# The transposed g through DRAM, probabilities normalised on GpSimd, and spread w_out steps in an attention and soft-MoE kernel

## The chip, the core and the metric

The kernel runs on one core of a Trainium2 chip. The metric is the device time of one execution in microseconds (us); smaller is better. The five engines of a core work side by side, each through its own list of instructions in order: PE (TensorE, matrix products), DVE (VectorE), ACT (ScalarE), POOL (GpSimd) and SP (SyncE, which here only issues DMAs). An instruction that waits holds up everything behind it in its engine's list.

## What is computed

Three layers follow one another. Attention runs within chunks of 64 tokens, for 8 heads of 64; its output x has 4608 tokens of 512. The second layer is a gated product, and the third routes tokens to 32 slots of 8 experts (soft MoE):

```python
attn = softmax(q @ k.T / 8)                      # within each chunk; sum + 1e-9 in the denominator
x = attn @ v
h = x @ w_in;  g = h * sigmoid(1.702 * h);  y = g @ w_out            # 512 -> 2048 -> 512
logits = y @ phi                                                     # 4608 x 32
d = softmax(logits over tokens);  c = softmax(logits over slots)
slot_out = relu((d.T @ y) @ w1[e]) @ w2[e]                           # per expert e
out = c @ slot_out
```

## The kernel before

The tokens are worked in 12 blocks of 384. For each block, `gemm(b, f)` computes 16 tiles of h (index f, 0 to 15), each 128 features by 384 tokens. Operands are split into a high and a low part, so one tile takes 12 matmuls (lines 240, 241, 242). ACT takes the tanh (line 244), and DVE makes `gt` from it (line 245), which holds g with features on partitions.

y is never formed. The logits come from `logits` with w_out and phi multiplied beforehand (line 301, tile `lp`). The slot inputs d.T @ y are gathered as d.T @ g, added into `acc` block by block by `dispatch` (line 398, tile `dtg`, 12 matmuls), and multiplied with w_out once at the end. For that product g must stand with tokens on partitions. DVE transposes each `gt` in squares of 32 by 32 (line 252) into a tile `g1`, one for a group of four f; when a group is complete, 16 DMAs of 48 KB rearrange it, SBUF to SBUF, into `g2` (line 262). Half of them are issued by POOL and half by SP, in the last blocks all by SP. `dispatch(b-1)` in block b reads the four `g2` tiles. The last block transposes on PE instead (`gemm_t`).

Attention for the blocks ahead is worked between the gemm tiles. One step `attn_a` takes 128 tokens: scores on PE (line 178, tile `s`), maximum and subtraction on DVE (183, 184), exponential on ACT (188), sum, small addition and reciprocal on DVE (190, 191, 193), and the multiplication by the reciprocal (194), on DVE for the steps taken here. `attn_b` transposes the result on PE (206) and copies it on ACT (208). `attn_c` multiplies with v on PE (224, tile `x`) and splits the output into `xh` (ACT, 230) and `xl` (DVE, 231), the operands of a later gemm. The PSUM tiles of `s` and `x` share one buffer (`pair_tile`, one buffer), so an `s` waits until the `xl` of the `x` before it is done, and an `x` until the subtraction (184) of the `s` before it.

`conv_wo` turns a 512 KB piece of w_out from float64 to float32: ACT (line 102), then DVE (103, 106). `load_wo` loads the next piece by SP (line 409). The two take turns.

What stands after which tile is given by the table `PLAN` (`LAST` for the last block): a letter for the step, a number for its part, and the f after which `side` calls it: `l` logits, `s` slots, `a`, `b`, `c` attention, `d` dispatch, `w` one step of w_out. SP issues in program order. The other engines' lists are ordered by a scheduler that estimates when operands are ready, so a step may stand well behind its f there. Tiles of 768 KB come from a pool `slab` of 10 buffers (`xh`, `xl`, `g1`, `g2`, and expert weights towards the end). `TABLE` says when expert weights are loaded into buffers that fall free in blocks 9 to 11.

Of the kernel before, what the change touches and what calls it, by code (L numbers as in the profile page):

```python
# [8 lines left out]
F32 = mybir.dt.float32  # L9
# [11 lines left out]
NM = 8  # L21
NSPARE = 6
NW = 17
NSP = 2
ROOM = {'w': 4, 's': 6, 'q': 4, 'v': 2, 'x': 2, 'p': 6}
TABLE = {'9.13': 'wxx', '10.6': 'q', '10.11': 'vq', '10.15': 'v', '11.0': 'ssw', '11.2': 's', '11.6': 's', 'a': 'ss', 'b': 'ssss', 'e': 'pppppp'}
TABLE.update({f'11.{f}': TABLE.get(f'11.{f}', '') + 'w' for f in range(1, 16)})
EVAC = 'vvvvvvvvvvvvvvaa'
LAST = (('l3', 1), ('s0', 2), ('d0', 4), ('l0', 4), ('s1', 6), ('l1', 8), ('l2', 12))


PLAN = (('l3', 1), ('s0', 2), ('w0', 2), ('a2', 4), ('d0', 4), ('l0', 4), ('b1', 4), ('c0', 4), ('w1', 6), ('s1', 6), ('a3', 8), ('l1', 8), ('b2', 8), ('c1', 8), ('w2', 10), ('w3', 11), ('a4', 12), ('l2', 12), ('b3', 12), ('c2', 12))
NCV = 6
FIRST = "q0 A0 q1 z Li0 A1 q2 Li1 q3 v0 Li2 i0 A2 B0 C0 v1 B1 C1 phi v2 i1 Li3 B2 C2 v3 A3 q4 Li4 i2 Li5 Li6 g0 Li7 g1 i3 Li8 i4 i5 q5 Li9 v4 i6 Li10 g2 g3 Li11 A4 i7 B3 g4 Li12 i8 C3 Lo0r q6 i9 g5 Li13 g6 i10 B4 q7 A5r Li14 i11 g7 o0 g8 i12 i13 g9 Lo1r C4 v5 Lo2r A6r Li15 i14 B5 Lo3 Lo4r i15 o1 g10 C5 g11 g12 g13 o2 Lo5r v6 Lo6 g14 Lo7r Lo8r s o3 g15 G0 o4 Lo9 Lo10r o5 Lo11r o6 G1 Lo12r A7 o7 Lo13r o8 G2 G3 v7 o9 B6 c0 o10 v8 Lo14 G4 o11 o12 C6 d0 G5 o13 c1 t0 Lo15 t1 o14 m0 G6 G7 G8 t2 t3 B7 d1 c2 q8 q9 G9 o15 t4 l0 d2 c3 G10 l1 C7 m1 l2 A8r G11 t5 d3 l3 t6 G12 v9 B8 t7 G13 S t8 G14 D1 t9 t10 t11 C8 t12 G15 T t13 t14 q10 m2 t15 D3 v10 A9 q11 B9 A10 q12"
EPS = 1e-9
# [3 lines left out]
def attention_moe_softmoe_kernel(  # L39
# [12 lines left out]
    nc = tc.nc  # L52
# [6 lines left out]
    NB = NT // T  # L59
# [7 lines left out]
    slab = ctx.enter_context(tc.tile_pool(name="slab", bufs=NSLAB))  # L67
    wpool = ctx.enter_context(tc.tile_pool(name="wpool", bufs=NW))
    mid = ctx.enter_context(tc.tile_pool(name="mid", bufs=NM))
    vpool = ctx.enter_context(tc.tile_pool(name="vpool", bufs=NV))  # L70
    st_p = ctx.enter_context(tc.tile_pool(name="st", bufs=2))
    ps_h = ctx.enter_context(tc.tile_pool(name="ps_h", bufs=3, space=bass.MemoryType.PSUM))
# [8 lines left out]
    def slab_tile(shape, dtype, name):  # L81
        return slab.tile(shape, dtype, tag="s", name=name)
# [153 lines left out]
    def gemm(b, f):  # L236
        h = ps_h.tile([128, T], F32, tag="h", name="h")
        for k in range(KD):
            a, l = w_t[f][:, 0, k, :], w_t[f][:, 1, k, :]
            nc.tensor.matmul(out=h, lhsT=a, rhs=xh[b][:, k, :], start=(k == 0), stop=False)  # L240
            nc.tensor.matmul(out=h, lhsT=a, rhs=xl[b][:, k, :], start=False, stop=False)  # L241
            nc.tensor.matmul(out=h, lhsT=l, rhs=xh[b][:, k, :], start=False, stop=(k == KD - 1))  # L242
        t = mid_tile([128, T], "gt") if b else pro[0].tile([128, T], F32, tag="gt", name="gt", bufs=NF)
        nc.scalar.activation(out=t, in_=h, func=ACTF.Tanh, scale=0.851)  # L244
        nc.vector.scalar_tensor_tensor(out=t, in0=t, scalar=1.0, in1=h, op0=ALU.add, op1=ALU.mult)  # L245
        gt[b, f] = t
        q, j = divmod(f, GF)
        if b in (0, NB - 1):
            return
        if j == 0:  # L250
            g1[q] = slab_tile([128, 4, NCP, GF * 32], F32, "g1")
        nc.vector.transpose(  # L252
            out=g1[q][:, :, :, 32 * j:32 * (j + 1)], in_=t.rearrange("p (a b c) -> p b a c", b=4, c=32)
        )
        if j == GF - 1:
            dst = slab_tile([128, 4, NCP, GF * 32], F32, f"g2_{q}")
            g2.setdefault(b, []).append([dst[:, :, i, :] for i in range(NCP)])
            src = g1.pop(q)
            for fq in range(4):
                for tb in range(4):  # L260
                    eng = nc.gpsimd if tb % 2 and b + NSP < NB else nc.sync
                    eng.dma_start(  # L262
                        out=dst[32 * tb:32 * tb + 32, fq].rearrange("p a c -> p (a c)"),
                        in_=src[32 * fq:32 * fq + 32, tb].rearrange("p a c -> p (a c)"),
                    )

    def gemm_t(b, f, g=None):
        g = gt[b, f] if g is None else g
# [123 lines left out]
    def dispatch(b):  # L392
        dt, cr = dt_t.pop(b)
        g = g2.pop(b)
        p = ps.tile([128, 512], F32, tag="m" if b + 1 < NB else "pt", name="dtg")
        for i in range(NCP):
            for j in reversed(range(4)):
                nc.tensor.matmul(  # L398
                    out=p[32 * j:32 * (j + 1)], lhsT=dt[:, i, :], rhs=g[j][i], start=(i == 0), stop=(i == NCP - 1)
                )  # L400
        nc.vector.scalar_tensor_tensor(out=acc, in0=acc, scalar=cr, in1=p, op0=ALU.mult, op1=ALU.add)
# [36 lines left out]
    def load(kind, eng):  # L438
        room, runs = ROOM[kind], []
        while units and (2 if units[0][0] == 1 else 1) <= room:  # L440
            u = units.pop(0)
            room -= 2 if u[0] == 1 else 1
            if runs and runs[-1][0] == u[:-1] and runs[-1][1] + runs[-1][2] == u[-1]:
                runs[-1][2] += 1
            else:
                runs.append([u[:-1], u[-1], 1])
        if not runs:
            return
        if kind == "x":
            wo_t["x"] = wo_t.get("x", 0) + 1  # L450
            t = wo_t["t"][:, wo_t["x"], :]
        else:
            alloc = {"w": w_tile, "s": slab_tile, "p": spare_tile, "v": v_alloc, "q": q_alloc}[kind]
            t = alloc([128, ROOM[kind] * DH], F32, "w12")
        at, live = 0, set()
        for key, c, m in runs:
            if key[0] == 1:
                v = t[:, at:at + m * DM].rearrange("p (c k f) -> p c k f", c=m, k=KD)
                at += m * DM
                eng.dma_start(out=v, in_=w1[:, key[1], c:c + m])  # L460
                for z in range(m):
# [23 lines left out]

    def at(key):
        for c in TABLE.get(key, ""):
            load(c, nc.gpsimd)

    def tail():  # L490
        b = NB - 1
# [128 lines left out]
    def side(b, f):  # L620
        for name, at in (LAST if b == NB - 1 else PLAN):
            if f != at:
                continue
            kind, i = name[0], int(name[1:])
            if kind == "l":
                if i == NG - 1:
                    logits(b - 1, i)
                else:
                    logits(b, i)
            elif kind == "s":  # L630
                (slots_a, slots_b)[i](b - 1)
            elif kind == "d":
                dispatch(b - 1)
            elif kind == "w":
                if 1 < b < 10:
                    more_wo()
            elif (b + 1) * NCP + i < NB * NCP:
                cp = (b + 1) * NCP + i
                if kind == "a":
                    attn_a(cp)  # L640
                    load_qk(cp + 2)
                elif kind == "b":
                    attn_b(cp)
                else:
                    attn_c(cp)
                    load_v(cp + 2)
# [118 lines left out]
```

## Time and profile before

| | us |
|---|---|
| median of 3 runs | 729.85 (726.99 to 732.1) |
| profiled execution | 733.41 |
| its span, first to last instruction | 731.6 |
| busy within the span: PE | 658.2 |
| DVE | 458.8 |
| ACT | 242.2 |
| POOL | 213.7 |

The granted clock of PE was 0.981 of full speed on average. In the views below a row of the timeline gives start, duration, engine, line, operation, tiles (out<-in), shapes and count, and in brackets the idle time of that engine ahead of it with what ended it. A matmul of float32 operands appears as two instructions, so the 12 of `dispatch` count 24. Successive matmuls overlap, so the time that one takes from PE is read from start to start. Blocks 2 to 11 start at 146.8, 206.4, 255.4, 303.2, 352.5, 401.0, 449.6, 499.2, 548.6 and 593.0 us; from 646 us to the end follow the experts and the output.

### The profile page before, as it was taken

What the parts mean: (1) busy time and instruction counts of PE and PEld (TensorE: products, weight loads), DVE (VectorE), ACT (ScalarE), POOL (GpSimd) and SP (SyncE); (2) the same over time, 40 slices, a digit from 0 to 9 for tenths busy, and PEclk for the clock granted to TensorE, in tenths of its full rate; (3) what the DMA queues carried; (4) which work ended last, traced back from release to release, by engine and by line L of the source; (5) the groups of instructions that cost most, each with busy time, mean ns of one, the idle gap of its engine ahead of it and who ended that gap; (6) DMA issues with size and microseconds to landing.
All of it is one profiled execution on the core that took longest, in us unless ns stands there. A gap on an engine that the chain in (4) does not pass through costs nothing.

```text
span 731.6 us, 17216 instructions
## 1 busy us (share of the span) xinstructions
PE 658.2 (90%) x6862; PEld 535.6 (73%) x6862; DVE 458.8 (63%) x988; ACT 242.2 (33%) x517; POOL 213.7 (29%) x400
## 2 busy tenths in 40 slices
PE   3878999999899999998999999989999988988873
PEld 2777976667796978887879788869687976846542
DVE  6798672658577686677777866767677544331033
ACT  4556344523332333323333333233233221121132
POOL 1335021222323342424232424242332023145410
PEclk9988999999999999999999999999999999999998
DMA  7846274254444645544446355444563366779996
GB/s 248 316 177 228 87 223 153 59 173 120 113 130 125 168 109 151 159 129 115 132 132 179 92 163 167 136 118 129 122 196 87 100 212 190 248 237 394 405 378 260
DMA packets 55216, 129.14 MB, mean 177 GB/s; under 512 B 14176, under 2 KB 25440, under 8 KB 55136
## 3 DMA queue, kind: packets, MB, share of 16 engines
q1 hardware_dynamic: 35568, 75.59, 33.1%
q0 software_dynamic: 19568, 52.45, 22.7%
q8 instruction: 54, 0.88, 0.5%
q14 instruction: 26, 0.21, 0.1%
HBM read 87.10 MB, written 9.44 MB: 132 GB/s over the span
## 4 chain that ended last, share of the span: by engine, by line
PE 64%; DVE 13%; DMA 9%; issue 4%; SPq 4%; ACT 4%; POOL 0%; DVEq 0%; ACTq 0%
PE h L240 13%; PE h L241 12%; PE h L242 12%; DMA wo<-in_moe_w_out_dram 5%; PE dtg L398 4%; PE lp L301 4%; SPq L262 4%; PE x L224 3%; DVE gt L245 2%; DMA g<-g 2%; PE h1p L555 2%; PE fp L575 2%; PE s L178 2%; PE op L603 2%; PE pt L206 2%
## 5 line engine op out<-in xcount | busy, mean ns | idle before, releaser
L240 PE MATMUL h<-xh,w 128*128 128x384 f32 x768 | 268.3, 350 | 0.7 <-ACT xh L230 0.7
L242 PE MATMUL h<-xh,w 128*128 128x384 f32 x768 | 260.5, 339 | 0.0
L241 PE MATMUL h<-xl,w 128*128 128x384 f32 x768 | 260.5, 339 | 0.0
L262 POOL DMA_DIRECT2D g<-g x288 | 141.2, 498 | 327.4 <-issue 101.5
L244 ACT ACTIVATE gt<-h 128x384 f32<-128x384 f32 x192 | 93.0, 489 | 212.9 <-PE h L242 212.1
L240 PEld LDWEIGHTS h<-xh,w 128*128 128x128 f32 x768 | 146.5, 191 | 14.0 <-issue 9.4
L245 DVE SCALAR_TENSOR_TENSOR gt<-gt,h 128x384 f32<-128x384 f32 x192 | 104.6, 545 | 74.7 <-ACT gt L244 74.0
L241 PEld LDWEIGHTS h<-xl,w 128*128 128x128 f32 x768 | 146.3, 190 | 1.9 <-issue 1.5
L242 PEld LDWEIGHTS h<-xh,w 128*128 128x128 f32 x768 | 146.0, 190 | 0.1
L252 DVE STREAM_TRANSPOSE g<-gt 128x384 f32<-128x384 f32 x160 | 91.9, 575 | 6.2 <-DMA g<-g 2.3
L301 PE MATMUL lp<-gt,wp 128*32 128x384 f32 x384 | 50.5, 496 | 5.5 <-DVE gt L245 5.5
L460 POOL DMA_DIRECT2D w<-in_moe_w_dram x41 | 21.8, 536 | 90.7 <-PE h L242 36.3
L224 PEld LDWEIGHTS x<-pt_sb,v 64*64 64x64 f32 x1152 | 22.4, 145 | 28.8 <-issue 24.4
L224 PE MATMUL x<-pt_sb,v 64*64 64x64 f32 x1152 | 27.0, 236 | 18.2 <-issue 9.3
L188 ACT ACTIVATE e<-e 128x512 f32<-128x512 f32 x36 | 22.7, 631 | 57.2 <-DVE e L184 57.2
L398 PE MATMUL dtg<-g,dt 128*32 128x512 f32 x264 | 32.3, 622 | 7.9 <-DVE gt L245 2.7
L178 PE MATMUL s<-qk 64*64 64x64 f32 x1152 | 27.5, 237 | 12.3 <-DMA qk<-in_qk_dram 7.9
L178 PEld LDWEIGHTS s<-qk 64*64 64x64 f32 x1152 | 22.3, 146 | 21.9 <-issue 15.1
L183 DVE TENSOR_REDUCE mx<-s 128x8 f32<-128x512 f32 x36 | 24.1, 669 | 17.8 <-PE s L178 17.7
L127 POOL TENSOR_TENSOR w<-cv,w 128x512 fp32r<-128x512 f32 x16 | 21.6, 1357 | 46.1 <-ACT w L126 38.9
L208 ACT ACTIVATE pt_sb<-pt 128x512 f32<-128x512 f32 x36 | 21.5, 596 | 40.2 <-PE pt L206 40.2
L190 DVE TENSOR_REDUCE sm<-e 128x8 f32<-128x512 f32 x36 | 24.5, 681 | 12.0 <-ACT e L188 12.0
(106 smaller groups left out, 607.9 us busy)
## 6 DMA issues: line engine op xcount, KB each, us to landing
w<-in_moe_w_dram POOLq DMA_DIRECT2D x47, 512.0 KB, 7.4
qk<-in_qk_dram SPq DMA_DIRECT2D x36, 512.0 KB, 4.8
g<-g SPq DMA_DIRECT2D x352, 48.0 KB, 2.3
g<-g POOLq DMA_DIRECT2D x288, 48.0 KB, 2.0
v<-in_v_dram SPq DMA_DIRECT2D x36, 256.0 KB, 4.7
stg<-in_moe_w_in_dram SPq DMA_DIRECT2D x16, 512.0 KB, 8.8
stg<-in_moe_w_out_t_dram SPq DMA_DIRECT2D x16, 512.0 KB, 5.2
wo<-in_moe_w_out_dram SPq DMA_DIRECT2D x16, 512.0 KB, 4.5
```

The costliest lines, as they stand in the source:

```text
L178: nc.tensor.matmul(out=p[w, h, hp, :], lhsT=t[r, 0, hp, w], rhs=t[r, 1, hp, w], start=True, stop=True)
L190: nc.vector.tensor_reduce(out=sm, in_=e, axis=AX.X, op=ALU.add)
L224: nc.tensor.matmul(out=x[64 * z:64 * z + 64, h, a, w], lhsT=t[r, 2 * a + z, w], rhs=p[r, 2 * a + z, w], start=True, stop=True,)
L240: nc.tensor.matmul(out=h, lhsT=a, rhs=xh[b][:, k, :], start=(k == 0), stop=False)
L241: nc.tensor.matmul(out=h, lhsT=a, rhs=xl[b][:, k, :], start=False, stop=False)
L242: nc.tensor.matmul(out=h, lhsT=l, rhs=xh[b][:, k, :], start=False, stop=(k == KD - 1))
L244: nc.scalar.activation(out=t, in_=h, func=ACTF.Tanh, scale=0.851)
L245: nc.vector.scalar_tensor_tensor(out=t, in0=t, scalar=1.0, in1=h, op0=ALU.add, op1=ALU.mult)
L252: nc.vector.transpose(out=g1[q][:, :, :, 32 * j:32 * (j + 1)], in_=t.rearrange("p (a b c) -> p b a c", b=4, c=32))
L262: eng.dma_start(out=dst[32 * tb:32 * tb + 32, fq].rearrange("p a c -> p (a c)"), in_=src[32 * fq:32 * fq + 32, tb].rearrange("p a c -> p ( ...
L301: nc.tensor.matmul(out=lp[b][32 * j:32 * (j + 1), :], lhsT=wp[:, f, :], rhs=gt[b, f], start=(g == 0), stop=(g == NG - 1),)
L398: nc.tensor.matmul(out=p[32 * j:32 * (j + 1)], lhsT=dt[:, i, :], rhs=g[j][i], start=(i == 0), stop=(i == NCP - 1))
```

## The change

It makes four edits.

- A complete group of g is written to a DRAM tile by 4 DMAs of 192 KB, all issued by SP (line 259 of the new kernel), in place of 16 DMAs of 48 KB by SP and POOL. A new step `g` (`load_g`) reads all four groups of block b-1 back in block b with 4 DMAs of 768 KB (line 271), tokens on partitions, after f = 3 (after f = 2 in the last block). The `g2` buffers are taken there, no longer as each group completes.
- `dispatch` moves from f = 4 to f = 8 in `PLAN` and from f = 4 to f = 6 in `LAST`.
- The attention steps called from `side` multiply by the reciprocal (line 194) on POOL.
- The w_out steps move from f = 2, 6, 10, 11 to f = 6, 7, 14, 15. In `TABLE`, the loads of block 9 come at f = 15 and from SP, and two slab loads of block 11 at f = 7 in place of f = 2 and f = 6.

```diff
-NSP = 2
-TABLE = {'9.13': 'wxx', ... '11.0': 'ssw', '11.2': 's', '11.6': 's', ...}
+TABLE = {'9.15': 'wxx', ... '11.0': 'ssw', '11.7': 'ss', ...}
-LAST = (('l3', 1), ('s0', 2), ('d0', 4), ('l0', 4), ('s1', 6), ('l1', 8), ('l2', 12))
+LAST = (('l3', 1), ('s0', 2), ('g0', 2), ('l0', 4), ('d0', 6), ('s1', 6), ('l1', 8), ('l2', 12))
-PLAN = (('l3', 1), ('s0', 2), ('w0', 2), ('a2', 4), ('d0', 4), ('l0', 4), ('b1', 4), ('c0', 4), ('w1', 6), ...
+PLAN = (('l3', 1), ('s0', 2), ('g0', 3), ('a2', 4), ('l0', 4), ('b1', 4), ('c0', 4), ('s1', 6), ('w0', 6), ('w1', 7), ...
...
         if j == GF - 1:
-            dst = slab_tile([128, 4, NCP, GF * 32], F32, f"g2_{q}")
-            g2.setdefault(b, []).append([dst[:, :, i, :] for i in range(NCP)])
-            src = g1.pop(q)
+            src, d = g1.pop(q), dram.tile([4, 32, 4, NCP * GF * 32], F32, tag="g", name="g_dram")
+            g_dram[b, q] = d
             for fq in range(4):
-                for tb in range(4):
-                    eng = nc.gpsimd if tb % 2 and b + NSP < NB else nc.sync
-                    eng.dma_start(
-                        out=dst[32 * tb:32 * tb + 32, fq].rearrange("p a c -> p (a c)"),
-                        in_=src[32 * fq:32 * fq + 32, tb].rearrange("p a c -> p (a c)"),
-                    )
+                nc.sync.dma_start(
+                    out=d[:, :, fq, :].rearrange("b p x -> p b x"),
+                    in_=src[32 * fq:32 * fq + 32].rearrange("p b a c -> p b (a c)"),
+                )
+    def load_g(b):
+        g2[b] = []
+        for q in range(NG):
+            t = slab_tile([128, 4, NCP, GF * 32], F32, f"g2_{q}")
+            nc.sync.dma_start(
+                out=t.rearrange("p q a c -> p (q a c)"), in_=g_dram.pop((b, q)).rearrange("b p q x -> (b p) (q x)")
+            )
+            g2[b].append([t[:, :, i, :] for i in range(NCP)])
...
-            load(c, nc.gpsimd)
+            load(c, nc.sync if key[0] == "9" else nc.gpsimd)
...
-                    attn_a(cp)
+                    attn_a(cp, True)
```

How the lists of the engines change is shown at three places of block 3 or 4; every block from 3 to 9 has the same pattern. On PE before, these rows of block 3 stand between the tiles f = 4 and f = 5 (`s` scores, `dtg` dispatch, `lp` logits, `pt` transpose, `x` the product with v):

```order
L178 MATMUL s<-qk 64x64 x16
L398 MATMUL dtg<-g_3_2390,dt 32x512
L398 MATMUL dtg<-g_2_2240,dt 32x512
L398 MATMUL dtg<-g_1_2089,dt 32x512
L398 MATMUL dtg<-g_0_1916,dt 32x512
...
L301 MATMUL lp<-gt,wp 32x384 x4
L206 MATMUL pt<-ident,e 128x128 x4
L224 MATMUL x<-pt_sb,v 64x64 x16
```

In the changed kernel the dispatch of block 3 stands after the tile f = 11, between the second `s` and the second `x` of the block; the third `s` follows after f = 12:

```order
L310 MATMUL lp<-gt,wp 32x384
L178 MATMUL s<-qk 64x64 x16
L407 MATMUL dtg<-g_3_2435,dt 32x512
L407 MATMUL dtg<-g_2_2433,dt 32x512
L407 MATMUL dtg<-g_1_2431,dt 32x512
L407 MATMUL dtg<-g_0_2429,dt 32x512
...
L224 MATMUL x<-pt_sb,v 64x64 x16
...
L178 MATMUL s<-qk 64x64 x16
L310 MATMUL lp<-gt,wp 32x384 x3
L206 MATMUL pt<-ident,e 128x128 x4
```

So the dispatch moved by seven tiles, and the second `s` from after f = 8 to after f = 11. On DVE before, this is what stands in block 3 around that second attention step, from its maximum to the `xl` of the `x` after it:

```order
L183 TENSOR_REDUCE mx<-s 128x8
L184 TENSOR_TENSOR e<-s,mx 128x2x4x64
L190 TENSOR_REDUCE sm<-e 128x8
L191 TENSOR_SCALAR sm<-sm 128x8
L193 RECIPROCAL rs<-sm 128x8
L194 TENSOR_TENSOR e<-e,rs 128x512
L231 TENSOR_TENSOR xl<-x,xh 128x2x2x128
```

In the changed kernel (block 4), two `gt`, three transposes, the addition into `acc` and a third `gt` stand between them, and the multiplication (194) is gone to POOL:

```order
L183 TENSOR_REDUCE mx<-s 128x8
L184 TENSOR_TENSOR e<-s,mx 128x2x4x64
L245 SCALAR_TENSOR_TENSOR gt<-gt,h 128x384 x2
L252 STREAM_TRANSPOSE g_3161<-gt 128x12x32
L190 TENSOR_REDUCE sm<-e 128x8
L252 STREAM_TRANSPOSE g_3161<-gt 128x12x32
L191 TENSOR_SCALAR sm<-sm 128x8
L410 SCALAR_TENSOR_TENSOR acc<-acc,cr,dtg 128x512
L193 RECIPROCAL rs<-sm 128x8
L245 SCALAR_TENSOR_TENSOR gt<-gt,h 128x384
L252 STREAM_TRANSPOSE g_3161<-gt 128x12x32
L231 TENSOR_TENSOR xl<-x,xh 128x2x2x128
```

The `xl` thus moved behind seven other instructions. On SP before, these rows issue the DMAs of block 4 from its first complete group of g on (`qk` and `v` feed attention):

```order
L262 DMA g_0_3111<-g_3021 32x384 x8
L161 DMA qk<-in_qk_dram 128x1024
L167 DMA v<-in_v_dram 128x512
L409 DMA wo_3259<-in_moe_w_out_dram 128x512
L262 DMA g_1_3284<-g_3144 32x384 x8
```

In the changed kernel the same stretch holds four writes, four reads and, after the second group, the load of w_out, whose conversion now stands seven tiles later:

```order
L259 DMA g_dram<-g_2895 32x4x384 x4
L271 DMA g_0_2987<-g_dram 128x1536
L271 DMA g_1_2989<-g_dram 128x1536
L271 DMA g_2_2991<-g_dram 128x1536
L271 DMA g_3_2993<-g_dram 128x1536
L161 DMA qk<-in_qk_dram 128x1024
L167 DMA v<-in_v_dram 128x512
L259 DMA g_dram<-g_3011 32x4x384 x4
L418 DMA wo_3143<-in_moe_w_out_dram 128x512
```

The writes and reads of g stand on SP alone, POOL's list has none of them any more, and the reads stand ahead of the block's `qk` and `v`.

## Rows read from the trace of the kernel before

**Rows 1.** Timeline of PE: start us, us, engine line op, count, [idle]; blocks 3 and 10.

```profile
218.22 0.70 PE L178 MATMUL s<-qk 64*64 64x64 f32 x32
219.36 2.78 PE L398 MATMUL dtg<-g,dt 128*32 128x512 f32 x24 [0.45 <-DVE gt L245]
221.94 0.86 PE L301 MATMUL lp<-gt,wp 128*32 128x384 f32 x8
222.72 0.66 PE L206 MATMUL pt<-ident,e 128*128 128x128 f32 x4
223.31 0.69 PE L224 MATMUL x<-pt_sb,v 64*64 64x64 f32 x32
...
561.61 2.78 PE L398 MATMUL dtg<-g,dt 128*32 128x512 f32 x24 [0.45 <-DVE gt L245]
```

**Rows 2.** Timeline of PE, block 4: the first and the thirteenth of undisturbed gemm matmuls.

```profile
301.16 0.33 PE L240 MATMUL h<-xh,w 128*128 128x384 f32 x1
...
303.24 0.34 PE L240 MATMUL h<-xh,w 128*128 128x384 f32 x1
```

**Rows 3.** Timeline of PE, block 3, after the tile f = 8.

```profile
232.46 0.69 PE L178 MATMUL s<-qk 64*64 64x64 f32 x32
...
234.88 0.83 PE L301 MATMUL lp<-gt,wp 128*32 128x384 f32 x2 [0.95 <-DVE gt L245]
...
237.94 0.69 PE L224 MATMUL x<-pt_sb,v 64*64 64x64 f32 x32 [0.59 <-DVE e L184]
238.57 0.45 PE L240 MATMUL h<-xh,w 128*128 128x384 f32 x1
```

**Rows 4.** Timeline of ACT, same stretch; then waits of blocks 3 to 9 (total, times, longest).

```profile
232.50 0.68 ACT L102 ACTIVATE wo<-wo 128x512 f32<-128x512 f32 x1 [3.60 <-DMA wo<-in_moe_w_out_dram]
...
ACT wo L102 <- DMA wo<-in_moe_w_out_dram: 34.7, 14, 4.0
```

**Rows 5.** Timeline of DVE, block 3: one attention step, then a gemm tile's two.

```profile
236.42 0.65 DVE L183 TENSOR_REDUCE mx<-s 128x8 f32<-128x512 f32 x1
237.10 0.69 DVE L184 TENSOR_TENSOR e<-s,mx 128x512 f32<-128x512 f32 x1
238.49 0.69 DVE L190 TENSOR_REDUCE sm<-e 128x8 f32<-128x512 f32 x1 [0.70 <-ACT e L188]
...
239.69 0.69 DVE L194 TENSOR_TENSOR e<-e,rs 128x512 f32<-128x512 f32 x1
240.30 0.68 DVE L231 TENSOR_TENSOR xl<-x,xh 128x512 fp32r<-128x512 f32 x1
240.90 0.54 DVE L245 SCALAR_TENSOR_TENSOR gt<-gt,h 128x384 f32<-128x384 f32 x1
241.48 0.58 DVE L252 STREAM_TRANSPOSE g<-gt 128x384 f32<-128x384 f32 x1
```

**Rows 6.** PE in block 2; then a window: length, busy (count) of PE, PEld, DVE, ACT, POOL, granted clock, DMA share, GB/s.

```profile
187.55 0.69 PE L224 MATMUL x<-pt_sb,v 64*64 64x64 f32 x32 [3.18 <-issue]
...
188.00:192.00 4.00, 4.00 (x32) 3.93 (x22) 3.44 (x8) 1.27 (x3) 0.00 (x0) 0.61 0.54 182
```

**Rows 7.** Timeline of PE, block 11.

```profile
602.85 0.45 PE L321 MATMUL lg<-lps,sel 128*128 128x384 f32 x1 [2.01 <-DVE lps L313]
...
611.18 4.46 PE L398 MATMUL dtg<-g,dt 128*32 128x512 f32 x24 [2.28 <-DMA g<-g]
```

**Rows 8.** SP's issues on line 262 (ns min/median/max, first to last); window of the weight stream.

```profile
L262 SPq DMA_DIRECT2D g<-g x352: 507/589/2149, 94.8 to 607.8; - x176
...
656.00:692.00 36.00, 31.64 (x526) 19.32 (x518) 4.88 (x17) 3.66 (x10) 18.77 (x36) 1.00 1.02 397
```

**Rows 9.** Groups by line and form: busy us, mean ns, idle before.

```profile
L106 DVE SCALAR_TENSOR_TENSOR cv<-stg,cv 128x512 uint32<-128x512 uint32 x32 | 26.2, 825 | 0.3
...
L106 DVE SCALAR_TENSOR_TENSOR wo<-wo,wo 128x512 uint32<-128x512 uint32 x16 | 10.7, 672 | 0.2
...
L194 POOL TENSOR_TENSOR e<-e,rs 128x512 f32<-128x512 f32 x3 | 4.1, 1354 | 0.0
```

More of the change, by code (lines that the diff above doesn't have):

```diff
@@ L23 @@
 NW = 17
-NSP = 2
 ROOM = {'w': 4, 's': 6, 'q': 4, 'v': 2, 'x': 2, 'p': 6}
-TABLE = {'9.13': 'wxx', '10.6': 'q', '10.11': 'vq', '10.15': 'v', '11.0': 'ssw', '11.2': 's', '11.6': 's', 'a': 'ss', 'b': 'ssss', 'e': 'pppppp'}
+TABLE = {'9.15': 'wxx', '10.6': 'q', '10.11': 'vq', '10.15': 'v', '11.0': 'ssw', '11.7': 'ss', 'a': 'ss', 'b': 'ssss', 'e': 'pppppp'}
 TABLE.update({f'11.{f}': TABLE.get(f'11.{f}', '') + 'w' for f in range(1, 16)})
 EVAC = 'vvvvvvvvvvvvvvaa'
-LAST = (('l3', 1), ('s0', 2), ('d0', 4), ('l0', 4), ('s1', 6), ('l1', 8), ('l2', 12))
-PLAN = (('l3', 1), ('s0', 2), ('w0', 2), ('a2', 4), ('d0', 4), ('l0', 4), ('b1', 4), ('c0', 4), ('w1', 6), ('s1', 6), ('a3', 8), ('l1', 8), ('b2', 8), ('c1', 8), ('w2', 10), ('w3', 11), ('a4', 12), ('l2', 12), ('b3', 12), ('c2', 12))
+LAST = (('l3', 1), ('s0', 2), ('g0', 2), ('l0', 4), ('d0', 6), ('s1', 6), ('l1', 8), ('l2', 12))
+PLAN = (('l3', 1), ('s0', 2), ('g0', 3), ('a2', 4), ('l0', 4), ('b1', 4), ('c0', 4), ('s1', 6), ('w0', 6), ('w1', 7), ('a3', 8), ('d0', 8), ('l1', 8), ('b2', 8), ('c1', 8), ('a4', 12), ('l2', 12), ('b3', 12), ('c2', 12), ('w2', 14), ('w3', 15))
 NCV = 6
@@ L69, in attention_moe_softmoe_kernel @@
     mid = ctx.enter_context(tc.tile_pool(name="mid", bufs=NM))
+    dram = ctx.enter_context(tc.tile_pool(name="dram", bufs=8, space=bass.MemoryType.DRAM))
     vpool = ctx.enter_context(tc.tile_pool(name="vpool", bufs=NV))
@@ L255, in gemm @@
         if j == GF - 1:
-            dst = slab_tile([128, 4, NCP, GF * 32], F32, f"g2_{q}")
-            g2.setdefault(b, []).append([dst[:, :, i, :] for i in range(NCP)])
-            src = g1.pop(q)
+            src, d = g1.pop(q), dram.tile([4, 32, 4, NCP * GF * 32], F32, tag="g", name="g_dram")
+            g_dram[b, q] = d
             for fq in range(4):
-                for tb in range(4):
-                    eng = nc.gpsimd if tb % 2 and b + NSP < NB else nc.sync
-                    eng.dma_start(
-                        out=dst[32 * tb:32 * tb + 32, fq].rearrange("p a c -> p (a c)"),
-                        in_=src[32 * fq:32 * fq + 32, tb].rearrange("p a c -> p (a c)"),
-                    )
+                nc.sync.dma_start(
+                    out=d[:, :, fq, :].rearrange("b p x -> p b x"),
+                    in_=src[32 * fq:32 * fq + 32].rearrange("p b a c -> p b (a c)"),
+                )
+    g_dram = {}
+    def load_g(b):
[6 more added lines that the diff above has]
+            g2[b].append([t[:, :, i, :] for i in range(NCP)])
     def gemm_t(b, f, g=None):
@@ L633, in side @@
                 dispatch(b - 1)
+            elif kind == "g":
+                load_g(b - 1)
             elif kind == "w":
```

## Prediction, made before the changed kernel was run

> **What bounds the kernel now.** I read the busy times first: PE works in 658.2 of 731.6 us, so it sets the end, and an edit is worth only what it takes from PE's work or from its idle time. So I went down PE's timeline from block to block. The dispatch of block 3 starts at 219.36 and that of block 10 at 561.61 [rows 1]: seven equal blocks (3 to 9) in 342.25 us, or 48.9 each.
>
> How much of that is PE's own work? Taken from start to start: twelve undisturbed gemm matmuls take 303.24 - 301.16 = 2.08 [rows 2], so 16 tiles 33.3. Four `lp` take 222.72 - 221.94 = 0.78, four groups 3.1; the four transposes `pt` 0.59, three times 1.8; the dispatch 221.94 - 219.36 = 2.58 [rows 1]. `x` takes 238.57 - 237.94 = 0.63 [rows 3], and `s`, which has as many matmuls and the same busy time, I give as much: three of each 3.8. The `lg` matmuls I put at 0.35 (two instructions of a gemm matmul's size). Sum 44.9, so 4.0 per block are lost.
>
> I looked for the 4.0 in the same rows. Dispatch: from `s` at 218.22 to `x` at 223.31 are 5.09, against 0.63 + 2.58 + 0.78 + 0.59 = 4.58 of work: 0.5 lost, behind a `gt`. After the tile f = 8: from `s` at 232.46 to the next tile at 238.57 are 6.11. Of work stand there `s`, `lp`, `pt`, `x`, and some six more gemm matmuls (1.04): 3.67. So 2.4 are lost [rows 3]. The last 1.0 is small change at f = 12 and between kinds of matmul.
>
> The 2.4 have one cause, seen on ACT: at 232.50 its line 102 has just waited 3.60 us for the DMA of a w_out piece, and in blocks 3 to 9 this wait comes 14 times with 34.7 us in all [rows 4]. ACT's list is in order, so the tanh behind it is late, then `gt` on DVE, then `lp` on PE [0.95]; the maximum of the second attention step starts at 236.42, four us after its `s` began [rows 3, 5], and `x`, which shares the buffer with that `s`, waits for the subtraction.
>
> **The change, part by part.** *The w_out steps.* Load and conversion now stand seven tiles or more apart, over 7 x 2.08 = 14.6 us. The row [rows 4] shows a piece arriving 3.6 us after ACT was ready for it. ACT's wait ends, and with it the 2.4 per block.
>
> *The dispatch.* Its 2.58 stay. What becomes late next? The third `s` stands after the tile f = 12 and needs the buffer of the second `x`, that is, its `xl` on DVE. On PE there lie between the second and the third `s`: dispatch 2.58, `x` 0.63, a tile 2.08, in all 5.3. On DVE, in its new order: maximum 0.68, subtraction 0.69, three `gt` at 0.54, three transposes at 0.58, sum 0.69, the two small operations about 0.5, the addition into `acc` about 0.7 (an operation of 128x512, as line 194), `xl` 0.68 [rows 5]. That is 7.3 if none overlaps the next; the starts in those rows lie 0.03 to 0.1 closer than the durations, so 6.8 to 7.2. PE thus waits 1.5 to 1.9 in a place where it did not; I take 1.6. Bounds: 0.8, if the scheduler's order leaves two small gaps less, and 2.3, if each step starts late by the 0.70 that the sum has behind the exponential [rows 5]. The 0.5 behind `gt` at the old dispatch goes, the small change stays near 0.9.
>
> *POOL's multiplication* takes 1.354 [rows 9] against 0.69 on DVE. It is hidden: it starts when the reciprocal is done, and DVE's third `gt`, transpose and `xl` (1.8) and the third `s` follow before PE comes to the transposes `pt`. Without that cover it costs 1.354 - 0.69 = 0.7, three times a block. POOL is free for it: the g DMAs it issued are gone from its list.
>
> *g through DRAM.* The trace has no DRAM write of this kind. SP issued half of 64 DMAs of g a block, 32, and issues 20 now (four groups of four writes, four reads), at 0.589 a median issue [rows 8]: 7 us less, on an engine that bounds nothing. The reads can be issued once the last group of the block before is transposed and written: about four tiles of work plus four issues into the block, 14 us; the dispatch stands about 31 us into the block. So 17 us for 3.15 MB (four times 768 KB), while the writes, as many bytes again, spread over the rest of the block. The two nearest rates: 397 GB/s in the weight stream [rows 8], by which the reads take 8 us, and 182 GB/s in a busy stretch of block 2 [rows 6], by which they take 17.3. I take the first, since DMAs there were as large as these and the second stretch was not short of DMA (share 0.54). Cost nothing; ends 0 and the case below.
>
> [...]
>
> *Blocks 3 to 9*: 44.9 + 1.6 + 0.9 = 47.4 for 48.9, a gain of 1.5, seven times 10.5.
>
> *Block 2.* Here the stall is 3.18 before an `x`, and in the 4 us behind it the granted clock is 0.61, between the levels 1.2 and 2.4 GHz: [rows 6] PE gave 4 us for 2.44 of work, 1.56 lost. Both go, 0.4 of small change too, and the new wait comes: -3.18 - 1.56 - 0.4 + 1.6 = -3.5.
>
> *Block 10* keeps its dispatch near its end: its last `xl` now stands behind dispatch and transposes on DVE, before the first tile of block 11, 1.1 later, less the 0.5 at the old dispatch: +0.6.
>
> *Block 11.* PE waits 2.01 for `lps` and 2.28 for a g DMA of the last group, after which the dispatch takes 4.46, not 2.78 [rows 7, 1]: 1.7 at the lower clock. The new list puts the dispatch two tiles later and the read of g behind writes that are long done: -2.01 - 2.28 - 1.7 + 0.5 for small waits that remain = -5.5.
>
> *Blocks 0, 1 and the tail*: nothing. Two slab loads of block 11 come up to 5 tiles later, but the stream that they belong to runs at 397 GB/s with PE idle only 4.4 of 36 us there [rows 8].
>
> *Sum*: -10.5 - 3.5 + 0.6 - 5.5 = -18.9. From the profiled 733.4 this is 714.5; the median of the runs is 3.6 below that execution, so 711.
>
> **Rivals.** *A: the new wait is long enough for the clock to fall.* For it: a stall of 3.18 and one of 2.28 shortly behind one of 2.01 were followed by the lower clock [rows 6, 7]. Against it: 2.01 alone was not. If the wait is 2.3 and each is followed by block 2's loss of 1.56, a block costs 2.3 more than I put, over blocks 2 to 9 18: 729, no change. DVE could be slowed by POOL's multiplication: line 106 takes 825 ns in the first blocks and 672 later [rows 9]. The Trainium skill, "SBUF — State Buffer", section "Who interferes with whom", says that a DVE instruction with two SBUF inputs contends with a GpSimd instruction that reads SBUF, and one with at most one does not; `gt`, the subtraction and `xl` have one input in PSUM, so by it this chain isn't touched.
>
> *B, the other side: the g read comes late.* It decides if the reads run under 3.15 MB / 17 us = 185 GB/s. For it: the 182 GB/s above, and that the reads share the DMA engines with qk, v and the writes. At 134 GB/s (about three quarters of it, the other traffic taken off) they take 23.5 us, the dispatch waits 6.2, and 1.6 of clock follow: 7.8 over nine blocks is +70, so 781. Against it: the DMA share of the stretch was half.
>
> *C: the change doesn't do what it says.* The w_out conversion still waits, since the load stands behind g's writes and reads on SP, which wait for DVE. Then the 2.4 stay beside the new 1.6, less the 0.5 and 0.1 of the rest: +1.0 in each of blocks 2 to 9, +0.6 in block 10 and -5.5 in block 11, so about 3 above before, 733. Against it: seven tiles, 14.6 us, are more than the SP list holds there.
>
> *D: the g traffic starves the expert weights* of block 11 and the tail: the reads and writes of the last two blocks, 6.3 MB at 397 GB/s, push 16 us of the stream; if half shows, 719; if all, 727 or more.
>
> **How the numbers follow.** The forecast has 0.66, A 0.13, B 0.11, C 0.06, D 0.04. The likeliest case's own range, with the wait at 0.8 or 2.3 in eight blocks (-6.4, +5.6) and the block 11 gain halved (+2.7), is 704 to 719. With A and D in and B out, the range is 703 to 730. A measurement of this kernel can tell about 1% (7.3 us) from no change. Faster than 722.5 are the forecast and half of D, with part of A: 0.70; within 1% the rest of A, C and D, and a B that is barely late: 0.18; slower 0.12, from B and a tail of D.
>
> **What would show it.** Right: ACT's wait on line 102 for the w_out DMA gone in blocks 3 to 9; blocks of about 47.4; PE's third `s` waiting 1.5 to 1.9 for DVE's `xl`, with the granted clock at 1.00 behind it; no `dtg` waiting for a DMA; block 11's waits of 2 us and the 4.46 gone. Wrong: a `dtg` that waits for g from DRAM (B); a granted clock under 0.7 behind the third `s` (A); line 102 still waiting (C); PE idle on expert weights behind 646 us (D); or `pt` waiting for POOL's multiplication, which I hold hidden.

## The result and the profile after

| | us |
|---|---|
| median of 4 runs, changed | 722.28 (721.42 to 722.89) |
| median of 4 runs, before, same chip | 729.49 |
| ratio | 0.990, 95% interval 0.9863 to 0.9937 |
| profiled execution, changed | 722.78 (before: 733.41) |
| its span | 721.0 (before: 731.6) |

The change makes the kernel 1% faster. The forecast was 711, with 703 to 730 as the range: the sign is right, the gain is 7 us where 18.9 were forecast. The profiled executions differ by 10.6, more than the medians, since the one before lay 3.9 above its median.

The page of the changed kernel, its busy times:

```profile
span 721.0 us, 16332 instructions
PE 661.4 (92%) x6830; PEld 530.0 (74%) x6830; DVE 432.7 (60%) x963; ACT 240.5 (33%) x517; POOL 95.2 (13%) x130
```

POOL has lost the issuing of the g DMAs (213.7 to 95.2), DVE the multiplication. PE is busy 3 us longer with 32 matmuls fewer (all in the first expert product): a sign that some of its waiting lies inside what the page counts as busy.

From block 3 on the timeline of PE shows one `lg` in each block, always after the tile f = 2, so the distance from one to the next is a block. First and last of blocks 3 to 9 (start us, us, engine, line, operation):

```profile
210.26 0.51 PE L330 MATMUL lg<-lps,sel 128*128 128x384 f32 x2
...
549.14 0.51 PE L330 MATMUL lg<-lps,sel 128*128 128x384 f32 x2
```

That is (549.14 - 210.26) / 7 = 48.41 per block; the same rows before stand at 213.62 and 555.86, 48.89 each. By stage, from the `lg` rows of both profiled executions:

| stage | before | after | difference | forecast |
|---|---|---|---|---|
| start to `lg` of block 2 | 161.6 | 160.6 | -1.0 | 0 |
| `lg` of block 2 to that of 3 | 52.0 | 49.6 | -2.4 | -3.5 |
| blocks 3 to 9 | 342.2 | 338.9 | -3.4 | -10.5 |
| block 10 | 44.7 | 45.7 | +1.0 | +0.6 |
| block 11 | 47.1 | 40.6 | -6.5 | -5.5 |
| from the last `lg` to the end | 84.0 | 85.6 | +1.7 | 0 |

So the error has one large place: blocks 3 to 9 give 0.5 each instead of 1.5.

Where do the 48.41 go? Block 5 on PE, the first attention step (compare [rows 1], where the dispatch stood between `s` and `lp`):

```profile
311.70 0.69 PE L178 MATMUL s<-qk 64*64 64x64 f32 x32
312.32 1.33 PE L310 MATMUL lp<-gt,wp 128*32 128x384 f32 x8
313.59 0.66 PE L206 MATMUL pt<-ident,e 128*128 128x128 f32 x4
...
315.32 0.69 PE L224 MATMUL x<-pt_sb,v 64*64 64x64 f32 x32 [0.38 <-issue]
```

The `lp` takes 313.59 - 312.32 = 1.27 instead of 0.78, and four gemm matmuls between `pt` and `x` take 1.32 instead of 0.69. DVE in the same stretch shows why:

```profile
309.47 1.12 DVE L361 STREAM_TRANSPOSE dt<-d 32x96 f32<-32x96 f32 x4 [0.20 <-ACT d L350]
310.61 1.16 DVE L369 STREAM_TRANSPOSE lt<-lg 32x96 f32<-32x96 f32 x4
...
312.22 0.55 DVE L245 SCALAR_TENSOR_TENSOR gt<-gt,h 128x384 f32<-128x384 f32 x1
...
313.79 0.68 DVE L183 TENSOR_REDUCE mx<-s 128x8 f32<-128x512 f32 x1
...
314.54 0.68 DVE L184 TENSOR_TENSOR e<-s,mx 128x512 f32<-128x512 f32 x1
```

DVE is without a pause from 309.47 on: first the small transposes of the routing, then the work of two tiles. The `gt` that the fourth `lp` needs ends at 312.77 and that matmul starts at 312.82; the maximum starts 1.4 us after its `s` has ended; the subtraction ends at 315.22 and `x`, which shares the buffer of `s`, starts at 315.32. So 0.49 + 0.63 = 1.1 are lost here. (The profile puts 0.38 of it down to "issue" and the rest inside busy time; that `x` waits for the subtraction is read from the times.)

Before, DVE was no quicker: in block 3 the same subtraction ended 3.81 after the start of its `s` (218.22 in [rows 1]), now it ends 3.52 after:

```profile
221.38 0.65 DVE L184 TENSOR_TENSOR e<-s,mx 128x512 f32<-128x512 f32 x1
```

But there the dispatch kept PE at work for 2.6 us at just this point, and `x` came 1.28 after the subtraction had ended. In blocks 3 to 9 `x` starts 1.3 to 1.5 behind the subtraction before, and 0.10 behind it in the changed kernel, in each of the seven.

The second and third attention steps, later in the same block (PE):

```profile
331.40 0.83 PE L310 MATMUL lp<-gt,wp 128*32 128x384 f32 x2
332.16 0.69 PE L178 MATMUL s<-qk 64*64 64x64 f32 x32
332.79 2.78 PE L407 MATMUL dtg<-g,dt 128*32 128x512 f32 x24
335.50 0.69 PE L224 MATMUL x<-pt_sb,v 64*64 64x64 f32 x32
336.12 0.45 PE L240 MATMUL h<-xh,w 128*128 128x384 f32 x1
...
339.28 0.69 PE L178 MATMUL s<-qk 64*64 64x64 f32 x32 [0.80 <-DVE xl L231]
339.91 0.85 PE L310 MATMUL lp<-gt,wp 128*32 128x384 f32 x6
340.69 0.66 PE L206 MATMUL pt<-ident,e 128*128 128x128 f32 x4
```

Two losses more. The tile between `x` and the third `s` takes 339.28 - 336.12 = 3.16 instead of 2.08, for the `xl`: 1.08, where 1.6 were forecast. And one `lp` stands alone at 331.40, the other three of its group at 339.91: the lone one holds PE for 332.16 - 331.40 = 0.76, three take 0.78, as four do. The split thus costs 0.76 a block. The three sum to 1.1 + 1.1 + 0.8 = 3.0 of the 3.5 that a block loses beside 44.9 of work.

### The profile page after: what moved, and what is told of

Its sections match the earlier page's. It is cut to its first block, busy times and chain, and to the rows that moved or that the text cites. A ratio compares the mean times of both kernels' runs of the same rounds, so it can differ in the third digit from the quotient of the medians.

```text
span 721.0 us, 16332 instructions
## 1 busy us (share of the span) xinstructions
PE 661.4 (92%) x6830; PEld 530.0 (74%) x6830; DVE 432.7 (60%) x963; ACT 240.5 (33%) x517; POOL 95.2 (13%) x130
## 5 line engine op out<-in xcount | busy, mean ns | idle before, releaser
L252 DVE STREAM_TRANSPOSE g<-gt 128x384 f32<-128x384 f32 x160 | 88.3, 566 | 2.0
L194 POOL TENSOR_TENSOR e<-e,rs 128x512 f32<-128x512 f32 x28 | 30.2, 1078 | 444.7 <-DVE rs L193 400.9
L310 PE MATMUL lp<-gt,wp 128*32 128x384 f32 x384 | 56.5, 498 | 1.6 <-DVE gt L245 1.1
L231 DVE TENSOR_TENSOR xl<-x,xh 128x512 fp32r<-128x512 f32 x36 | 24.1, 670 | 16.1 <-ACT xh L230 16.0
L407 PE MATMUL dtg<-g,dt 128*32 128x512 f32 x264 | 30.6, 596 | 1.4 <-DVE dt L357 1.4
L230 ACT ACTIVATE xh<-x 128x512 fp32r<-128x512 f32 x36 | 21.5, 596 | 28.6 <-PE x L224 28.6
L206 PEld LDWEIGHTS pt<-ident,e 128*128 128x128 f32 x144 | 16.2, 147 | 20.0 <-issue 16.3
```

Of the source, the lines that this page charges most:

```text
L194: (nc.gpsimd if pool else nc.vector).tensor_tensor(out=e, in0=e, in1=rs.to_broadcast([128, 2 * KD, 64]), op=ALU.mult)
L252: nc.vector.transpose(out=g1[q][:, :, :, 32 * j:32 * (j + 1)], in_=t.rearrange("p (a b c) -> p b a c", b=4, c=32))
L310: nc.tensor.matmul(out=lp[b][32 * j:32 * (j + 1), :], lhsT=wp[:, f, :], rhs=gt[b, f], start=(g == 0), stop=(g == NG - 1),)
L407: nc.tensor.matmul(out=p[32 * j:32 * (j + 1)], lhsT=dt[:, i, :], rhs=g[j][i], start=(i == 0), stop=(i == NCP - 1))
```

## The experiments

All runs are of the whole kernel. Blocks 0 and 1 differ between the ten profiles by up to 5 us: the `lg` of block 2 starts anywhere from 158.8 to 164.6, with the same work ahead of it but for the way g is moved in block 1. The two latest (e2, e6) have a granted clock of 0.95 over the first 158 us, the others 0.96 to 0.98, and executions of one kernel differ as much (e2: 721.7 to 729.0, with a mean clock of 0.984 and 0.975). So kernels are compared by the length of blocks 3 to 9 as well as by their median. Each ratio is to runs of the kernel before in the same round, whose median was 729.5, 732.7 (e1 to e4), 731.0 (e5 to e7) and 730.2 (e8).

| kernel | median | ratio to before, interval | blocks 3 to 9, each |
|---|---|---|---|
| changed | 722.3 | 0.990 (0.986 to 0.994) | 48.41 |
| e1_w_only | 717.5 | 0.980 (0.975 to 0.985) | 47.38 |
| e2_after_w_old | 722.5 | 0.986 (0.981 to 0.991) | 48.24 |
| e3_after_no_pool | 723.4 | 0.988 (0.983 to 0.992) | 48.42 |
| e4_read_pool | 713.3 | 0.974 (0.969 to 0.978) | 47.02 |
| e5_x_later | 710.5 | 0.972 (0.968 to 0.976) | 46.54 |
| e6_w_old | 723.6 | 0.989 (0.984 to 0.995) | 47.89 |
| e7_last_sp | 710.9 | 0.975 (0.968 to 0.981) | 46.31 |
| e8_change_x_later | 716.9 | 0.985 (0.978 to 0.992) | 47.69 |

**The w_out steps alone.** The edit to the kernel before:

```diff
-... ('w0', 2) ... ('w1', 6) ... ('w2', 10), ('w3', 11) ...
+... ('w0', 6) ... ('w1', 7) ... ('w2', 14), ('w3', 15) ...
-TABLE = {'9.13': 'wxx', ...
+TABLE = {'9.15': 'wxx', ...
```

> The kernel before with the w_out steps spread as in the change (f = 6, 7, 14, 15; the loads of block 9 at f = 15) and nothing else. My theory after the comparison: this edit alone carries the gain, and the other three cost time. Blocks 3 to 9 lost 4.0 us each beside 44.9 of PE's work, 2.4 of them behind line 102; without that wait 7 x 2.3 = 16 go, and about 3 in block 2: 729.5 - 19 = 711. Rival 1: the 2.4 had another cause than the wait on line 102, and the change won by moving the dispatch: 729, no change. Rival 2: the wait only moves to the new places: 722 to 729.

Measured: 717.5, a ratio of 0.980, where the whole change has 0.990 (and its near relatives e2 and e3, in the same round as e1, 0.986 and 0.988): one and a half to two times its gain. Blocks go from 48.89 to 47.38, block 2 (by `lg` rows) from 52.0 to 47.6. The waits of ACT in blocks 3 to 9 (total us, times, longest) against the 34.7 of [rows 4]:

```profile
ACT wo L102 <- DMA wo<-in_moe_w_out_dram: 18.2, 14, 2.8
```

Half of the wait is left, though `PLAN` has seven tiles between load and conversion. SP issues one piece at 278.73, and ACT has come to it before it lands:

```profile
278.73 0.53 SPq L409 DMA_DIRECT2D wo<-in_moe_w_out_dram  x1
...
282.65 0.66 ACT L102 ACTIVATE wo<-wo 128x512 f32<-128x512 f32 x1 [0.93 <-DMA wo<-in_moe_w_out_dram]
```

They stand 3.9 us apart in time, not 14.6: SP comes to the load late, behind eight DMAs of g that wait for DVE, and the conversion stands early in ACT's list. The measured gain lies between my theory and rival 2: the wait on line 102 did cause the stall, and the spread takes away about half of it.

**The changed kernel with the w_out steps where they were.**

```diff
-... ('w0', 6), ('w1', 7) ... ('w2', 14), ('w3', 15))
+... ('w0', 2) ... ('w1', 6) ... ('w2', 10), ('w3', 11) ...
```

> The changed kernel with the w_out steps back at f = 2, 6, 10, 11. My theory: line 102 waits for its DMA again and holds the tanh, about 2 us in each of blocks 2 to 9: 722 + 16 = 738, slower than before the change. Rival: with half as many g DMAs on SP the w_out piece comes in time wherever its steps stand, so 722.

Measured: 722.5, and 48.24 a block, as the change. My theory was wrong and the rival's time right. Line 102 waits for no DMA in blocks 3 to 9. One piece in this kernel:

```profile
272.94 2.57 SPq L271 DMA_DIRECT2D g<-g_dram  x4
...
276.73 0.36 SPq L418 DMA_DIRECT2D wo<-in_moe_w_out_dram  x1
...
291.54 0.68 ACT L102 ACTIVATE wo<-wo 128x512 f32<-128x512 f32 x1
```

The conversion stands 14.8 us behind its load, and in the changed kernel 296.27 - 282.23 = 14.0, whichever f `PLAN` names; the piece lands 5 to 12 us after its issue here. The rival's reason (that it arrives in time) is thus not the whole of it: it is ACT's list that gives it the time. So the other three edits together had already ended the wait that the spread was to end. Which of them did, and why the scheduler then puts the conversion so much later, was not tested. e1 and e3 both have the spread and no multiplication on POOL, and e1 still waits while e3 does not, so g through DRAM or the move of the dispatch is needed for it.

**POOL's multiplication undone** (`attn_a(cp, True)` to `attn_a(cp)`).

> The changed kernel with the multiplication by the reciprocal (line 194) on DVE again. My theory: the multiplication stands ahead of the xl for which PE's third s waits (0.8 us now), so that wait grows by 0.7 in blocks 3 to 9 and 2: 722 + 5.5 = 728. Rival 1: DVE has a gap there, and nothing changes: 722. Rival 2: POOL's slower multiplication (1.08 us against 0.69) is itself on the path of the transposes, and DVE is better: 718.

Measured: 723.4 and 48.42 a block: nothing, so my 728 is missed. The third `s` waits 0.82 instead of 0.80. DVE's rows of block 5 say where the 0.69 went:

```profile
337.74 0.68 DVE L194 TENSOR_TENSOR e<-e,rs 128x512 f32<-128x512 f32 x1
338.34 0.68 DVE L231 TENSOR_TENSOR xl<-x,xh 128x512 fp32r<-128x512 f32 x1
338.94 0.57 DVE L252 STREAM_TRANSPOSE g<-gt 128x384 f32<-128x384 f32 x1
```

With the multiplication on DVE again, the list has a transpose of g behind `xl` that stands ahead of it in the changed kernel (there at 338.08, `xl` at 338.58). One takes the other's place, and `xl` ends at the same time. Rival 1 holds in its time, by another mechanism than a gap.

**The reads of g issued by POOL**, in the changed kernel:

```diff
         for q in range(NG):
...
-            nc.sync.dma_start(
+            nc.gpsimd.dma_start(
```

> The changed kernel with the four reads of g (line 271) issued by POOL instead of SP, ahead of nothing that feeds attention. In the order of PE the second s then stands after f = 8 again with the dispatch right behind it, its x too, the lp of f = 8 in one piece, and the third s waits for no xl that is behind three gt. My theory: the reads on SP ahead of qk made the list drift by three tiles, and the drift costs a lone lp (0.8) and the wait of s (1.1) per block: 48.4 becomes about 46.6, in all 722 - 14 = 708, with the 1.1 at f = 4 still there. Rival: the dispatch, three tiles earlier, waits for g (reads take 8 us from about 15 us into the block, the dispatch comes at 22): 1 to 4 us a block, 716 to 745.

Measured: 713.3 and 47.02 a block, 1.4 less than the change where 1.8 were expected. PE's rows at the second attention step of block 5:

```profile
318.02 0.69 PE L178 MATMUL s<-qk 64*64 64x64 f32 x32
318.95 2.78 PE L407 MATMUL dtg<-g,dt 128*32 128x512 f32 x24 [0.24 <-DMA g<-g_dram]
321.52 0.86 PE L310 MATMUL lp<-gt,wp 128*32 128x384 f32 x8
322.31 0.66 PE L206 MATMUL pt<-ident,e 128*128 128x128 f32 x4
322.89 0.69 PE L224 MATMUL x<-pt_sb,v 64*64 64x64 f32 x32
```

In blocks 3 to 6 the second `s` is back after f = 8 with the dispatch behind it (in 7 to 9 it comes 0.8 to 3.1 later); in all seven the four `lp` stand together and no `s` waits for an `xl`. The theory holds for most of the time that the drift costs. Its reason doesn't hold. In the changed kernel these rows of SP have the reads ahead of a `qk`:

```profile
292.51 0.72 SPq L161 DMA_DIRECT2D qk<-in_qk_dram  x1
...
315.62 3.38 SPq L271 DMA_DIRECT2D g<-g_dram  x4
319.10 0.39 SPq L161 DMA_DIRECT2D qk<-in_qk_dram  x1
```

But a `qk` is loaded two attention steps ahead: the one at 319.10 is for the third `s` of the block (339.28) and landed 9.5 us later, in time. The second `s` (332.16) uses the one issued at 292.51, which landed after 4.7, more than 30 us too soon. So no operand that the trace shows held the second `s` back. Its buffer would have, for part of the way: the `xl` of the first `x`, after which the buffer is free, ends only at 327.09, since the `xh` that it reads comes late on ACT.

```profile
325.75 0.59 ACT L230 ACTIVATE xh<-x 128x512 fp32r<-128x512 f32 x1
326.44 0.65 DVE L231 TENSOR_TENSOR xl<-x,xh 128x512 fp32r<-128x512 f32 x1
```

That `xh` starts 10.4 us after its `x` in each of the seven blocks of the changed kernel, 0.8 to 1.0 after it before, and 2.8 to 9.0 in e4. From 327.09 to the `s` at 332.16 another 5.1 pass for which the trace shows no reason but the list, which has `s` behind f = 11. With POOL issuing the reads the list has both earlier. What in the scheduler's estimates does it stays open.

The rival (that g is late for the earlier dispatch) shows only as 0.2 us in all of blocks 3 to 9. POOL's rows tell why:

```profile
291.11 1.75 POOL L271 DMA_DIRECT2D g<-g_dram  x3
...
312.53 0.59 POOL L271 DMA_DIRECT2D g<-g_dram  x1
```

Three of the four reads are issued in the block before, where groups 0 to 2 are already written, and only one is left for the block itself. It lands after 6.3 us, at 318.8, and the dispatch starts at 318.95. From SP, with all four in the block, the last was there at 317.9 + 9.4 = 327.3: a dispatch after f = 8, 17.4 us behind the `lg` as in e4, would have come at 324.5 and waited some 3 us for it.

**The logits and the first `x` one tile later**, on top of e4:

```diff
-... ('l0', 4), ('b1', 4), ('c0', 4), ...
+... ('l0', 5), ('b1', 5), ('c0', 5), ...
```

> e4_read_pool with l0, b1 and c0 at f = 5 instead of f = 4. My theory: where the dispatch stood, PE now waits for DVE, which at this point works off the small transposes of the routing; lp (0.5) and x (0.6) lose 1.1 per block, since no dispatch lies between s and lp any more. One tile later DVE is through: blocks 2 to 10 are 0.9 to 1.1 shorter, 713 - 9 = 704. Rival: the loss moves to the next step (the second s waits for the later xl, or the lp in front of it), 710 to 713.

Measured: 710.5, blocks of 46.54; five of the seven are 0.7 shorter than in e4, block 3 by 0.2, block 5 is 0.4 longer. Rows of block 5:

```profile
304.13 0.69 PE L178 MATMUL s<-qk 64*64 64x64 f32 x32
...
307.05 0.85 PE L310 MATMUL lp<-gt,wp 128*32 128x384 f32 x8
307.83 0.66 PE L206 MATMUL pt<-ident,e 128*128 128x128 f32 x4
308.42 0.69 PE L224 MATMUL x<-pt_sb,v 64*64 64x64 f32 x32
```

The `lp` takes 0.78, and `x` follows `pt` after 0.59, as it did behind the dispatch before. The 1.1 are gone; about 0.3 come back in the change from a gemm tile to other work and in `pt`, which now stands directly ahead of `x`. In this block the dispatch, now earlier by that much, waits 1.41 for g. The theory's mechanism holds, with 0.7 in most blocks where 0.9 to 1.1 were expected; its 704 is missed, and the rival's 710 to 713 met in time, though no loss moved to the second `s` or the `lp` ahead of it.

**The same edit on the changed kernel alone.**

> The changed kernel with l0, b1 and c0 at f = 5 instead of f = 4, nothing else; the second s still stands after the tile f = 11. My theory: of the 4.2 that PE loses per block in the change, 1.1 stand between the first s and its x, because the dispatch no longer lies there while DVE works off the routing's transposes. They go, the lone lp (0.6) and the wait of the third s (1.1) stay: blocks 3 to 9 take 47.4 instead of 48.4, 722 - 8 = 714. Rival: the later x delays what follows on DVE, and the wait of the third s takes over: 720 to 722.

Measured: 716.9, between the theory's 714 and the rival's 720, and all seven blocks at 47.69, 0.72 under the change. `x` now starts 0.76 behind the subtraction instead of 0.10. The wait of the third `s` is unchanged:

```profile
PE s L178 <- DVE xl L231: 5.6, 7, 0.8
```

So the loss where the dispatch had stood is a cost of its own, independent of the drift of the second `s`. The two corrections add up: 0.7 here and 1.4 from e4 make 2.1. e5, which has both, is 1.9 under the change with its wait for g in block 5, and e7, without that wait, 48.41 - 46.31 = 2.1.

**The w_out steps where they were, on top of e4.**

> e4_read_pool with the w_out steps back at f = 2, 6, 10, 11. My theory after e2: it isn't the f in PLAN that keeps line 102 from waiting but where ACT's list has it; with g through DRAM it stands 15 us behind the load in either case, so line 102 waits for nothing and the time is that of e4 within 3: 711 to 716. Rival: without the reads on SP ahead of it the conversion follows its load by 4 us again, as before, and the waits of 2 to 4 us are back: 725.

Measured: 723.6, so my 711 to 716 is missed and the rival's 725 nearly met, for neither reason. Line 102 waits for no DMA here either. Between the two profiles lie 11.5 us. Of these 4.9 lie ahead of block 2's `lg`, where the two kernels do the same and the granted clock was 0.95 instead of 0.98, and 6.1 in blocks 3 to 9, which take 47.89 instead of 47.02. There PE's waits name the dispatch, and 1.5 us more an `lp` that waits for `gt`:

```profile
PE dtg L407 <- DMA g<-g_dram: 3.4, 3, 2.2
```

The three are blocks 3 to 5. In each of them SP issues the load of a w_out piece 0.4 to 0.9 us ahead of POOL's last read of g, and that read lands after 6.8 to 8.4 us, in e4's blocks 3 to 5 after 5.0 to 6.3. So the places of the w_out loads matter to e4 through the reads of g. That the one load slows the other is read from these times; no run moves it alone.

**The last block's reads issued by SP**, on top of e5:

```diff
-            nc.gpsimd.dma_start(
+            (nc.sync if b == NB - 2 else nc.gpsimd).dma_start(
```

> e5_x_later with the four reads of the last block issued by SP, as in the change. My theory: in e4's last block the dispatch waited 1.0 for a read and lone lp and small pieces cost another 1.0; from SP they are gone: 1 to 2 under e5. Rival: from there on the stream of expert weights sets the end, and whatever PE gains in block 11 is given back: the same as e5 within 1.

Measured: 710.9, as e5 by the medians. In the profiles block 11 is 40.9 long instead of 41.6, and the stretch behind it 85.8 instead of 85.9, so 0.8 is gained and kept there, less than the 1 to 2 expected and not given back as the rival has it. That is less than the medians can tell. e5 and e7 are the fastest kernels of the study, about 1.5 to 2% faster than the changed one.

## Why the prediction was wrong

**What bounds the kernel, and the cause of its largest loss.** Right. PE is the bound. The 2.4 after f = 8 came from line 102: in the changed kernel that wait is gone and so is the loss, and e1, which moves nothing but the w_out steps and halves the wait, shortens the block by 1.5.

**The w_out steps.** The size was right, the edit it was put down to only in part. I took the f of `PLAN` for the place of the conversion ("seven tiles or more apart, over 7 x 2.08 = 14.6 us"). The 14 us are there in the trace, but e2 has them with the old f too, and e1 has 3.9 with the new. `PLAN` gives an earliest place for the engines that the scheduler orders; the distance that counts is that of the load in SP's list and the conversion in ACT's.

**The dispatch.** This is the step that failed. I wrote "The 0.5 behind `gt` at the old dispatch goes" and asked what is late next only at its new place. What the dispatch had covered at its old place I did not ask. It had given DVE 2.6 us to work off the routing's transposes; without it PE loses 1.1 between the first `s` and its `x`. So the term of -0.5 was +0.6 in truth, and e8 gives 0.72 of it back by a single edit. No run puts the dispatch alone back to f = 4; that its cover is what went is shown by the kernel before and e1, which have it there and `x` well behind the subtraction (mostly 1.3 us), and by e4 and the change, which don't and have 0.10. The clue stood in [rows 1]: `x` at 223.31 followed `pt` with no wait, while in [rows 3], with only `lp` and `pt` ahead of it, `x` waited for the subtraction (though there line 102 had made DVE late as well).

**The drift of the second `s`.** I saw it in the order and costed its wait, but not what it split. The order printed ahead of the prediction has one `lp` ahead of the second `s` and three behind the third; I counted `lp` by the group at 0.78 and didn't ask what a lone one costs. It costs as much as four: 0.76 a block, 5.3 in seven, put at nothing in the forecast. The wait for `xl` was the right mechanism, 1.08 instead of 1.6: DVE's chain from the maximum to the end of `xl` takes 6.3 where I had summed 6.8 to 7.2.

Together, per block: -0.5 (s) + 1.1 (first `x`) + 0.8 (lone `lp`) - 0.4 (small change) = +1.0 over the forecast of 47.4, which makes 7 us in seven blocks. That is the whole miss in blocks 3 to 9; the small change of 0.5 is what is left of the 3.5, not a measurement of its own. Block 2, 1.1 short of its forecast, was not taken apart.

**POOL's multiplication.** Hidden, as forecast; e3 shows it is worth nothing either way. It takes 1.08 on average (30.2 us for 28), less than the 1.354 that I used. The `xl` that lie wholly beside it take 0.69 us, the same ones in e3, with POOL idle, 0.68; no `gt` lies more than 0.25 us beside it. On that point the Trainium skill, "SBUF — State Buffer", section "Who interferes with whom", by which a DVE instruction with at most one SBUF input, outside the 2-port modes (a tensor-tensor operation like `xl` has none), doesn't contend with GpSimd, agrees with this trace.

**g through DRAM.** Right: no `dtg` waits for a DMA in blocks 3 to 9. The last read of block 5 lands at 327.3 and the dispatch is at 332.79, so 5.5 us were to spare, though the four reads took 11.7 from the first issue to the last landing where I had 8. What the detour costs is indirect: with the reads on SP the scheduler's list is a worse one (e4).

**Blocks 10 and 11.** Block 11 came out as forecast (-6.5 for -5.5): no `lps` wait, no wait for g, and the dispatch at a granted clock of 1.00:

```profile
594.80 0.51 PE L330 MATMUL lg<-lps,sel 128*128 128x384 f32 x2
...
621.50 2.78 PE L407 MATMUL dtg<-g,dt 128*32 128x512 f32 x24
```

Block 10 gave +1.0 for +0.6. The tail, forecast at nothing, gives 1.7 back. It lies behind the first output product: from there to the end the kernel before takes 38.2 and e1 37.2, the eight kernels with g through DRAM 39.9 to 41.1. What does it stays open.

**The rivals.** A did not come: the wait was shorter than forecast, and PE's granted clock was 1.00 in the 4 us behind it (window as in [rows 6]):

```profile
339.28:343.30 4.02, 4.02 (x79) 3.07 (x83) 2.94 (x5) 1.12 (x2) 0.00 (x0) 1.00 0.93 211
```

B, C and D did not come either: no dispatch waits, line 102 doesn't wait, block 11 is shorter. (B's sum has a slip: 23.5 - 17 is 6.5, not 6.2, which makes 784.) The true course was none of the four: several small losses at places that an edit uncovers, each under the size at which I had looked for one.

**The median.** I carried the profiled execution's gain over to the median. The execution of before that was profiled lay 3.9 above its median, the one of the changed kernel 0.5. So of the 11.3 by which 711 missed, 8.3 lie in the profiles (722.8 for 714.5), 7 of them in blocks 3 to 9, and about 3 in this step, which has nothing to do with the mechanism.

## What to carry to other kernels

When a block of work is moved, cost its old place too: list what the other engines did under its cover and what waits for them once it is gone. Where a scheduler orders the engines, read the distance between a load and its use from the lists and the trace, not from the table; and before putting a gain down to one edit, run that edit alone, since here one of four alone gave more than all four together. The same goes for the queue of a transfer: four reads issued by POOL instead of SP gave another list on PE, 1.4 us a block shorter.

## What the runs showed of the hardware

Four `lp` matmuls of 128x384 (two instructions each), each into its own 32 partitions of the result, take 0.78 us of PE together, and one alone takes 0.76 (331.40 to 332.16 in the changed kernel). Where a group had to wait for its fourth `gt`, its first three started within 0.02 us of each other (at 312.3). Products of this kind run side by side, so a group that is split costs PE the whole group's time again.

A 192 KB write to DRAM landed after 3.1 us and a 768 KB read after 8.0, both medians, with up to four in flight and other loads beside them. Issued by POOL, three of four a block earlier (e4), the same reads landed after 6.2. In blocks 3 to 9 of the changed kernel a 512 KB load issued right behind the four reads landed after 9.1 to 10.9, the other loads of its kind after 4.1 to 6.2.
